# Attention and SwiGLU on one core: the first unit's k cut in three around the first scores, DMA transposes ahead of the q/k loads, the second weight slice's loads at fixed points

## The chip, the core and the metric

The kernel runs on one NeuronCore of a Trainium2 chip. The engines named here are TensorE (PE; its weight loads are listed apart as PEld), VectorE (DVE), ScalarE (ACT), GpSimd (POOL) and SyncE (SP), which only issues transfers to the 16 DMA engines. The metric is device microseconds (us) of one execution. Before: 575.25 us, the median of three runs (572.65, 576.69, 575.25).

## The reference

Four batches of twelve heads with 448 positions and 64 columns go through a sigmoid attention; the result, normalized by its root mean square, goes through a SwiGLU block (768 to 1536 to 768):

```python
scores = scale * np.matmul(q, k.transpose(0, 1, 3, 2)) - np.log(S)
attn = 1.0 / (1.0 + np.exp(-scores))
attn_out = np.matmul(attn, v)
x = attn_out.transpose(0, 2, 1, 3).reshape(B * S, H * D)
xn = x / np.sqrt(np.mean(x * x, axis=-1, keepdims=True) + 1e-06) * rms_g
g, val = xn @ w_gate, xn @ w_val
out = (g / (1.0 + np.exp(-g)) * val) @ w_out
```

All inputs and the output are float32. The kernel keeps that precision by splitting each operand into a high and a low float16 half and taking three products of halves.

## The kernel before, in words

**Units and chunks.** The attention is cut into 12 units of four heads. A unit has 7 chunks of 64 key rows per head. For each chunk PE makes the scores (line 277, 12 matmuls in float16 halves), ACT puts the sigmoid on them (line 281), and two chunks later PE multiplies by v (line 292, 8 matmuls in float32). The loop takes chunks in pairs: two chunks of scores, then the two `av` products of the pair before. The loop variable `n` counts chunks in steps of two, so unit u begins at chunk 7u: unit 4 with `n` = 28, unit 7 in the second chunk of `n` = 48.

**How q and k reach PE.** Scores need q and k with the head column on the partitions, while the loads bring positions there. A unit's raw q or k is loaded by two transfers, one per head pair (line 190). DVE makes the halves (`qk_hi`, line 222, and `qk_lo`, line 226, two instructions). From unit 3 on one DMA transpose on SP turns all four halves of a unit (`transpose_both`, line 229; 28 blocks of 128x128 in float16). Units 1 and 2 use PE for all or part of it (`on_pe`, line 258). Unit 0 is turned on PE in float32 (`transpose_here`, line 247): q in two pieces of 4 and 3 blocks, then k the same way; each piece is evicted by ACT (line 251, the high half) and DVE (line 252, the low half). Ahead of that and between q and k, PE does filler matmuls (`warm`, line 871).

**What sets the order.** Nothing is scheduled by a tool: each engine runs its instructions in the order in which the code issues them. `FILL[c]` lists what is issued at chunk c of every unit u. Before, chunk 3 issues `qk_lo` of q for unit u+2 and then the k load for unit u+4; chunk 4 issues the q load for unit u+4 and then the DMA transposes for unit u+2. SP's queue takes these strictly in that order, and a transfer that waits holds all that stand behind it. A transfer also waits for the one issued eight earlier.

**Weights.** The weights of gate and value come in six slices of 256 columns. A slice has six loads (line 459; one of 384 KB and two of 192 KB for gate, the same for value). DVE rebuilds float32 from the words loaded (lines 439 to 441), forms differences (line 491), ACT and DVE make halves (lines 494, 497). The second slice's loads enter a list once DVE has been given the first slice. Before, the attention loop takes `n // LOADS_FROM` of the list at the end of every pair from n = 10 on; the split of the second slice is issued from n = 30 on.

**Normalization.** After a batch's three units, PE sums squares (`ssq`, line 349), DVE makes the inverse root (lines 354 to 377), PE spreads it over the partitions (`rinv`, line 387), ACT evicts it (line 388), and DVE scales x and makes sums and differences (lines 391, 413) whose halves ACT (line 395) and DVE (line 402) write. These parts stand in a list that is drained between chunks in an order fixed by costs in the code; each engine's order is thus fixed in the program, and they come ahead of the parts that split the weights only as their turn allows. The SwiGLU part (line 527 and later) follows.

Of the kernel before, what the change touches and what calls it, by code (L numbers as in the profile page):

```python
# [12 lines left out]
AF = mybir.ActivationFunctionType  # L13
ALU = mybir.AluOpType


SQ = 2.0**6
# [7 lines left out]
def attention_then_swiglu(  # L25
# [21 lines left out]
    nc = tc.nc  # L47
    B, H, S, D = q.shape
    DFF, DM = w_out.shape
    P = 128  # L50
    NPAIR = H // 2
    NSLOT = 2 * S // P
# [14 lines left out]
    ps_s = ctx.enter_context(tc.tile_pool(name="ps_s", bufs=2, space=bass.MemoryType.PSUM))  # L67
    ps_m = ctx.enter_context(tc.tile_pool(name="ps_m", bufs=4, space=bass.MemoryType.PSUM))

    WARM, BETWEEN = 6, 2  # L70
    SPLIT_AT, REST_AT = (8, 30), 12
    LOADS_FROM = 10
    NAT = (0, 2, 0, 1, 2, 0, 1, 2, 0, 1, 0, 1)
    PIECES = (0, 4), (4, 3)
    MID = 3
    SLOT = 0.8
    ACT_SLOT = 0.18

# [7 lines left out]
    ident = const.tile([P, P], F32, name="ident")  # L86
# [38 lines left out]
    t_b = [words(xc_room, XW + (2 + n) * UW, 2, 2, NSLOT, P, dt=F16) for n in range(3)]  # L125
# [47 lines left out]
    def bank(name):  # L173
        return ps_m.tile([P, 512], F32, tag="m", name=name)
# [4 lines left out]
    stt = nc.vector.scalar_tensor_tensor  # L179
# [3 lines left out]
    at, pav = {}, {}  # L183
# [8 lines left out]
    def load_qk(u, t):  # L192
        load((q, k)[t], (raw_b if u < 2 else ld_b)[u % 2][:, t], u)

    def load_v(u):
        load(v, v_b[u % 2], u)

# [17 lines left out]
    def raw(u, t):  # L215
        return (raw_b if u < 2 else ld_b)[u % 2][:, t]
# [20 lines left out]
            in_=nat(u)[:, t].rearrange("p l c d -> p (l c d)"),  # L237
        )

    def transpose_here(u, t):  # L240
        src, dst = raw(u, t), t_b[u % 3][:, t]
        ps = [bank("tr") for _ in range(2)]
        for c in range(NSLOT):
            half_, at = divmod(c, MID + 1)
            for r in range(2):
                o = ps[half_][D * r : D * r + D, at * P : at * P + P]
                nc.tensor.matmul(o, src[:, r, c], ident, start=True, stop=True)  # L247
        for half_ in range(2):
            n = MID + 1 - half_
            hi, lo = (dst[:, l, half_ * (MID + 1) : half_ * (MID + 1) + n].rearrange("p c r -> p (c r)") for l in range(2))  # L250
            nc.scalar.activation(hi, ps[half_][:, : n * P], AF.Copy, scale=SQ)
            stt(lo, ps[half_][:, : n * P], SQ, hi, ALU.mult, ALU.subtract)

    def on_pe(u, t, begin, n):
        for l in range(2):
# [69 lines left out]
    def run_evictions(n):  # L325
        for part in evictions[:n]:
            part()
        del evictions[:n]
# [123 lines left out]
    loads = []  # L452
# [8 lines left out]
    def run_load():  # L461
        if loads:
            loads.pop(0)[1]()
# [364 lines left out]
    K, Q = 1, 0  # L828
# [9 lines left out]
    def from_1(n, part, *t, cost=0.0):  # L838
        run = ahead_by(n, part, *t, cost=cost)
        return lambda u: u and run(u)  # L840

    def first(*parts):
        return [only(0, x, *a, cost=cost) for x, *a, cost in parts]

    def second(*parts):
        return [only(1, x, *a, cost=cost) for x, *a, cost in parts]

    FILL = (
        first((qk_hi, 1, Q, 0.53), (qk_lo, 1, Q, 1.0)) + second((qk_hi, 2, Q, 0.53), (qk_lo, 2, Q, 1.0), (load_qk, 4, Q, 0.0), (on_pe, 1, K, *PIECES[1], 0.0)) + [from_1(2, qk_hi, K, cost=0.53)],
        first((qk_hi, 1, K, 0.53), (qk_lo, 1, K, 1.0)) + [from_1(2, qk_lo, K, cost=1.0)],  # L850
        [from_1(2, qk_hi, Q, cost=0.53)],
        first((on_pe, 1, Q, *PIECES[0], 0.0)) + [from_1(2, qk_lo, Q, cost=1.0), from_1(4, load_qk, K)],
        first((on_pe, 1, Q, *PIECES[1], 0.0), (qk_hi, 2, K, 0.53)) + [from_1(4, load_qk, Q), from_1(2, transpose_both)],
        first((on_pe, 1, K, *PIECES[0], 0.0), (qk_lo, 2, K, 1.0)) + second((on_pe, 2, Q, *PIECES[0], 0.0)),
        first((transpose, 2, K, 0.0), (load_qk, 4, K, 0.0)) + second((on_pe, 2, Q, *PIECES[1], 0.0)),
    )
# [8 lines left out]
    with tc.manual_schedule():  # L865
# [3 lines left out]
        def warm(n):  # L869
            for _ in range(n):  # L870
                nc.tensor.matmul(ps_w[:, :P], ones, ones, start=True, stop=True)  # L871

        warm(WARM)
        load_qk(0, Q)
        load_qk(0, K)
        load_v(0)
        load_qk(1, Q)
        load_qk(1, K)
# [8 lines left out]
            for _ in range(3):  # L887
                run_load()

        transpose_here(0, Q)  # L890
        warm(BETWEEN)
        transpose_here(0, K)

        todo = [(u, c) for u in range(NU) for c in range(NSLOT)]
        split = {}
        for n in range(0, len(todo) + 2, 2):
            for u, c in todo[n : n + 2]:
                scores(u, c)
                run_evictions(1)
                for part in FILL[c]:  # L900
                    part(u)
                if n == 6 and c == 6:
                    g_columns()
                run_later()
            for u, c in todo[max(n - 2, 0) : n]:
                av(u, c)
                run_evictions(1)
                run_later()
            for _ in range(n // LOADS_FROM):
                if loads and loads[0][0] < 2:  # L910
                    run_load()
            if n in SPLIT_AT:
                fc = SPLIT_AT.index(n)
                split[fc] = split_w(fc)
                first, second = split[fc]
                splits.extend(first[:4] if fc == 0 else first + second)
            if n == REST_AT:
                splits.extend(split[0][0][4:] + split[0][1])
# [49 lines left out]
        for fc, n in order:  # L968
# [5 lines left out]
            elif fc + 1 < NFC:  # L974
                first, second = split[fc + 1] = split_w(fc + 1) if n == 0 else split[fc + 1]
# [97 lines left out]
```

## Time and profile before

| what | value |
|---|---|
| median of three runs | 575.25 us (572.65 to 576.69) |
| the profiled execution | 576.9 us, span 575.1 us |
| PE busy | 565.1 us (98%), in 4230 instructions |
| DVE busy | 437.8 us (76%) |
| ACT busy | 265.7 us (46%) |
| chain that ended last | PE 90%, ACT 4%, DVE 2%, DMA 2% |
| attention (0 to 140 us) | PE busy 134.47 us, DMA share 0.92 |
| rest (140 to 575 us) | PE busy 430.64 us, DMA share 0.46 |

The profile is of one execution that took 576.9 us; its span is 1.8 us shorter. Times of rows count from the start of the span. A row of the timeline gives start, duration, engine, line, operation, result and operands, how many instructions are merged in it, and in brackets how long the engine was idle ahead of it and what ended the idle time. "SPq" rows are the time that SP took to issue a transfer; the landing is later and told by another view. PEclk is the granted clock of TensorE as a part of 2.4 GHz.

### The profile page before, as it was taken

Reading aid. Unit: us, or ns where it says so; the run is one execution under the profiler, and the core shown is the slowest. Engines: PE = TensorE matmul, PEld = TensorE weight load, DVE = VectorE, ACT = ScalarE, POOL = GpSimd, SP = SyncE. Lnnn points to the kernel's source line nnn. Section 1 sums busy time; section 2 is a strip of 40 time slices with the busy share of each in tenths; the row PEclk is TensorE's granted clock in tenths of the full one; section 3 lists DMA queues with packets and bytes.
Section 4 is the critical chain, followed back from the end, with each engine's and each line's share of the span. In section 5 each row is a group of like instructions: output and inputs, shape, how many; then the busy total and the mean of one; then the engine's idle time right before and its main releaser. Section 6 shows DMA issues by size and latency. Waiting matters only on the chain.

```text
span 575.1 us, 10260 instructions
## 1 busy us (share of the span) xinstructions
PE 565.1 (98%) x4230; PEld 304.9 (53%) x4230; DVE 437.8 (76%) x576; ACT 265.7 (46%) x397; POOL 0.7 (0%) x6
## 2 busy tenths in 40 slices
PE   8998999999999999999999999999999999999997
PEld 6454554454555555555555555555556666666664
DVE  4786899998887777878778787787557987777751
ACT  5687698886454243342433424325438342222220
POOL 0000000000000000000000000000000000000000
PEclk9999899999999999999999999999999999999999
DMA  8999998980016357282563835632526566444211
GB/s 254 257 260 241 251 255 200 176 191 18 1 47 171 118 156 196 91 225 78 156 192 98 218 80 158 188 106 66 177 59 225 152 220 198 149 142 144 69 43 41
DMA packets 98417, 87.25 MB, mean 152 GB/s; under 512 B 38719, under 2 KB 91458, under 8 KB 98370
## 3 DMA queue, kind: packets, MB, share of 16 engines
q1 hardware_dynamic: 97810, 85.91, 56.0%
q8 instruction: 33, 0.54, 0.4%
q10 hardware_dynamic: 560, 0.69, 0.3%
q14 instruction: 14, 0.11, 0.1%
HBM read 61.34 MB, written 16.52 MB: 135 GB/s over the span
## 4 chain that ended last, share of the span: by engine, by line
PE 90%; ACT 4%; DVE 2%; DMA 2%; issue 1%; ACTq 0%; DVEq 0%
PE cb L527 28%; PE cd L527 14%; PE av L292 7%; PE oc L730 7%; PE od L730 7%; PE o L730 7%; PE ca L527 7%; PE sc L277 6%; PE ob L730 4%; ACT room L281 3%; DMA xc<-room 2%; PE ssq L349 1%; PE tr L247 1%; PE warm L871 1%; ACT wr L494 1%
## 5 line engine op out<-in xcount | busy, mean ns | idle before, releaser
L527 PEld LDWEIGHTS <-wr 128*128 128x128 f16 x1512 | 147.9, 98 | 138.6 <-issue 1.0
L527 PE MATMUL cb<-xc,wr 128*128 128x448 f16 x756 | 147.3, 352 | 0.0
L281 ACT ACTIVATE room<-sc 128x896 f32<-128x896 f32 x84 | 75.4, 934 | 18.5 <-PE sc L277 17.8
L292 PE MATMUL av<-room 64*64 64x448 f32 x672 | 72.4, 547 | 0.0
L527 PE MATMUL cd<-xc,wr 128*128 128x448 f16 x324 | 65.2, 352 | 0.0
L277 PE MATMUL sc<-xc 64*64 64x448 f16 x1008 | 58.6, 356 | 4.4 <-DMA xc<-room 2.3
L277 PEld LDWEIGHTS <-xc 64*64 64x64 f16 x1008 | 30.6, 108 | 37.1 <-issue 23.2
L582 DVE TENSOR_TENSOR room<-cd,room 128x448 f32<-128x448 f32 x24 | 15.0, 625 | 43.1 <-PE cd L527 43.1
L730 PEld LDWEIGHTS <-xc 128*128 128x128 f16 x360 | 35.2, 98 | 23.3
L497 DVE SCALAR_TENSOR_TENSOR wr<-wr 128x1536 f16<-128x1536 f32 (+3 forms) x28 | 37.3, 1355 | 10.7 <-ACT wr L494 10.7
L527 PE MATMUL ca<-xc,wr 128*128 128x448 f16 x216 | 44.8, 352 | 0.0
L730 PE MATMUL o<-room,wr 128*128 128x384 f16 x252 | 41.1, 326 | 0.0
L550 ACT ACTIVATE room<-cb 128x448 f32<-128x448 f32 x24 | 13.1, 544 | 53.8 <-PE cb L527 53.8
L292 PEld LDWEIGHTS av<-room 64*64 64x64 f32 x672 | 25.2, 135 | 23.3 <-issue 18.6
L571 ACT ACTIVATE room<-cb 128x448 f32<-128x448 f32 x24 | 13.1, 544 | 50.6 <-PE cb L527 30.6
L730 PEld LDWEIGHTS <-room 128*128 128x128 f16 x270 | 26.4, 98 | 17.5
L494 ACT ACTIVATE wr<-wr 128x768 f16<-128x768 f32 (+1 forms) x48 | 34.0, 761 | 0.0
L585 ACT ACTIVATE room<-room 128x448 f32<-128x448 f32 x24 | 13.8, 577 | 43.2 <-DVE room L582 43.2
L730 PEld LDWEIGHTS <-wr 128*128 128x128 f16 x252 | 24.7, 98 | 16.3
L685 ACT ACTIVATE xc<-xc 128x1536 f16<-128x1536 f32 (+1 forms) x12 | 14.5, 1260 | 35.7 <-DVE xc L682 35.7
L491 DVE TENSOR_TENSOR wr<-wr 128x384 f32<-128x384 f32 x48 | 26.5, 553 | 0.8
L543 ACT ACTIVATE room<-cb 128x448 f32<-128x448 f32 x24 | 13.1, 545 | 25.5 <-PE cb L527 25.5
(98 smaller groups left out, 681.3 us busy)
## 6 DMA issues: line engine op xcount, KB each, us to landing
y_d<-room SPq DMA_DIRECT2D x24, 448.0 KB, 3.2
xc<-in_moe_w_out_dram SPq DMA_DIRECT2D x12, 768.0 KB, 5.6
xc<-y_d SPq DMA_DIRECT2D x22, 384.0 KB, 4.4
room<-in_v_dram SPq DMA_DIRECT2D x24, 224.0 KB, 3.9
out_dram<-room SPq DMA_DIRECT2D x49, 96.0 KB, 2.2
wr<-in_moe_w_gate_dram SPq DMA_DIRECT2D x12, 384.0 KB, 4.2
wr<-in_moe_w_gate_dram SPq DMA_DIRECT2D x24, 192.0 KB, 4.8
wr<-in_moe_w_val_dram SPq DMA_DIRECT2D x12, 384.0 KB, 5.7
```

The lines of the kernel that those rows point to most:

```text
L277: nc.tensor.matmul(o, T[rows, 1, l, c, cols], T[rows, 0, m, :, cols], start=(n == 0), stop=(n == 2))
L281: nc.scalar.activation(a, ps[:, :, :S], AF.Sigmoid, bias=-math.log(S), scale=1.0 / (math.sqrt(D) * SQ * SQ))
L292: nc.tensor.matmul(ps[D * (j ^ r) : D * (j ^ r) + D, :S], v_b[u % 2][rows, r, c], a[rows, r], start=(c == 0), stop=(c == NSLOT - 1),)
L491: first.append((lambda o=o, f0=f0, f1=f1: tt(wf[:, o], wf[:, f0], wf[:, f1], ALU.subtract), 0.6))
L494: nc.scalar.activation(t[:, 0, s], wf[:, s], AF.Copy, scale=SW)
L497: stt(t[:, 1, s], wf[:, s], SW, t[:, 0, s], ALU.mult, ALU.subtract)
L527: nc.tensor.matmul(ps, w[:, l, b, c], xc[n, a][:, r, c], start=(not more and c == 0 and m == 0), stop=(c == NK - 1 and m == 2), skip_group ...
L543: nc.scalar.activation(y[:, 0], pb[:, :S], AF.Copy)
L582: tt(y[:, 1], pd[:, :S], y[:, 1], ALU.add)
L585: nc.scalar.activation(y[:, 1], y[:, 1], AF.Silu, scale=UNIT)
L685: return lambda: nc.scalar.activation(s[:, 0, a:b], f[:, a:b], AF.Copy), 0.0, ()
L730: nc.tensor.matmul(ps[:, :HALF], a(m, l), w(m, r), start=(not more and m == 0 and n == 0), stop=(m == NM - 1 and n == 2), skip_group_check ...
```

## The change

Three things change.

1. Unit 0's first loads are cut by blocks in place of head pairs: q in pieces of blocks 0-3 and 4-6, k in pieces of 0-1, 2-4 and 5-6, both head pairs in one transfer. PE turns q and the first piece of k, then runs the first chunk's scores; the second piece of k is turned behind chunk 0, the third behind chunk 1. The filler goes from six and two matmuls to five and none.
2. From unit 1 on, chunk 3 issues the DMA transposes of unit u+2, and chunk 4 the k and q loads of unit u+4.
3. The second weight slice's loads are taken at n = 18 and 20 (one each) and n = 26 and 28 (two each).

```diff
-    WARM, BETWEEN = 6, 2
+    WARM = 5
     SPLIT_AT, REST_AT = (8, 30), 12
-    LOADS_FROM = 10
+    LOADS_AT = {18: 1, 20: 1, 26: 2, 28: 2}
...
-    MID = 3
+    K_PIECES = (0, 2), (2, 3), (5, 2)
...
+    def load_first(t, *pieces):
+        rows = (q, k)[t][0, :4].rearrange("(r h) s d -> r (h s) d", r=2).rearrange("r (p c) d -> p r c d", p=P)
+        for begin, n in pieces:
+            nc.sync.dma_start(raw(0, t)[:, :, begin : begin + n], rows[:, :, begin : begin + n])
...
-    def transpose_here(u, t):
-        src, dst = raw(u, t), t_b[u % 3][:, t]
-        ps = [bank("tr") for _ in range(2)]
-        for c in range(NSLOT):
-            half_, at = divmod(c, MID + 1)
-            for r in range(2):
-                o = ps[half_][D * r : D * r + D, at * P : at * P + P]
-                nc.tensor.matmul(o, src[:, r, c], ident, start=True, stop=True)
...
+    def transpose_here(t, *pieces):
+        src, dst = raw(0, t), t_b[0][:, t]
+        ps = [bank("tr") for _ in pieces]
+        for o, (begin, n) in zip(ps, pieces):
+            for c in range(n):
+                for r in range(2):
+                    nc.tensor.matmul(
+                        o[D * r : D * r + D, c * P : c * P + P], src[:, r, begin + c], ident, start=True, stop=True
+                    )
+        for o, (begin, n) in zip(ps, pieces):
+            hi, lo = (dst[:, l, begin : begin + n].rearrange("p c r -> p (c r)") for l in range(2))
+            nc.scalar.activation(hi, o[:, : n * P], AF.Copy, scale=SQ)
+            stt(lo, o[:, : n * P], SQ, hi, ALU.mult, ALU.subtract)
...
-        first((qk_hi, 1, Q, 0.53), (qk_lo, 1, Q, 1.0)) + second(...
+        first((transpose_here, K, K_PIECES[1], 0.0), (qk_hi, 1, Q, 0.53), (qk_lo, 1, Q, 1.0)) + second(...
-        first((qk_hi, 1, K, 0.53), (qk_lo, 1, K, 1.0)) + [from_1(2, qk_lo, K, cost=1.0)],
+        first((transpose_here, K, K_PIECES[2], 0.0), (qk_hi, 1, K, 0.53), (qk_lo, 1, K, 1.0)) + [from_1(2, qk_lo, K, cost=1.0)],
...
-        first((on_pe, 1, Q, *PIECES[0], 0.0)) + [from_1(2, qk_lo, Q, cost=1.0), from_1(4, load_qk, K)],
-        first((on_pe, 1, Q, *PIECES[1], 0.0), (qk_hi, 2, K, 0.53)) + [from_1(4, load_qk, Q), from_1(2, transpose_both)],
+        first((on_pe, 1, Q, *PIECES[0], 0.0)) + [from_1(2, qk_lo, Q, cost=1.0), from_1(2, transpose_both)],
+        first((on_pe, 1, Q, *PIECES[1], 0.0), (qk_hi, 2, K, 0.53)) + [from_1(4, load_qk, K), from_1(4, load_qk, Q)],
...
-        load_qk(0, Q)
-        load_qk(0, K)
+        load_first(Q, *PIECES)
+        load_first(K, *K_PIECES)
...
-        transpose_here(0, Q)
-        warm(BETWEEN)
-        transpose_here(0, K)
+        transpose_here(Q, *PIECES)
+        transpose_here(K, K_PIECES[0])
...
-            for _ in range(n // LOADS_FROM):
-                if loads and loads[0][0] < 2:
-                    run_load()
+            for _ in range(LOADS_AT.get(n, 0)):
+                run_load()
```

On SP, between the transposes of unit 3 and those of unit 4, this stood before (`in_k`, `in_q`: loads of unit 6; `in_v`: units 3 and 4):

```order
L229 DMA_TRANSPOSE xc<-room 128x28x128
L459 DMA wr<-in_moe_w_gate_dram 128x3x256
L459 DMA wr<-in_moe_w_gate_dram 64x3x256
L190 DMA room<-in_v_dram 128x448 x2
L459 DMA wr<-in_moe_w_gate_dram 64x3x256
L190 DMA xc<-in_k_dram 128x448 x2
L459 DMA wr<-in_moe_w_val_dram 128x3x256
L190 DMA xc<-in_q_dram 128x448 x2
L229 DMA_TRANSPOSE xc<-room 128x28x128
L459 DMA wr<-in_moe_w_val_dram 64x3x256 x2
L190 DMA room<-in_v_dram 128x448 x2
```

The last transpose of these rows is that of unit 4. In the changed kernel the transposes of unit 4 come first of the following rows, and the second transpose is that of unit 5:

```order
L234 DMA_TRANSPOSE xc<-room 128x28x128
L190 DMA xc<-in_k_dram 128x448 x2
L190 DMA xc<-in_q_dram 128x448 x2
L464 DMA wr<-in_moe_w_gate_dram 128x3x256
L464 DMA wr<-in_moe_w_gate_dram 64x3x256
L190 DMA room<-in_v_dram 128x448 x2
L234 DMA_TRANSPOSE xc<-room 128x28x128
L190 DMA xc<-in_k_dram 128x448 x2
L190 DMA xc<-in_q_dram 128x448 x2
L464 DMA wr<-in_moe_w_gate_dram 64x3x256
L464 DMA wr<-in_moe_w_val_dram 128x3x256
L190 DMA room<-in_v_dram 128x448 x2
```

Behind these stand the last two value loads of the second slice and then the transposes of unit 6. The third gate load and all value loads have moved behind the transposes of unit 5; between the transposes of units 3 and 4 only q, k and v loads are left.

On ACT, from the first eviction on, before (lines 251 and 281 are the evictions of turned pieces and the sigmoids of chunks):

```order
L251 ACTIVATE xc<-tr 128x512
L251 ACTIVATE xc<-tr 128x384
L251 ACTIVATE xc<-tr 128x512
L251 ACTIVATE xc<-tr 128x384
L281 ACTIVATE room<-sc 128x896 x4
```

And in the changed kernel (lines 256 and 286):

```order
L256 ACTIVATE xc<-tr 128x512
L256 ACTIVATE xc<-tr 128x384
L256 ACTIVATE xc<-tr 128x256
L286 ACTIVATE room<-sc 128x896
L256 ACTIVATE xc<-tr 128x384
L286 ACTIVATE room<-sc 128x896
L256 ACTIVATE xc<-tr 128x256
L286 ACTIVATE room<-sc 128x896 x2
```

The sigmoid of chunk 0 has moved ahead of two of k's three evictions, that of chunk 1 ahead of one. On DVE the low half of k's third piece now stands behind the halves of unit 1's q; after these first rows the orders of PE, ACT and DVE are the same as before.

## Rows read from the trace of the kernel before

**Rows 1.** The chain that ended last, 36 to 64 us: start, us, what.

```profile
44.62 9.59 DMA xc<-room
```

**Rows 2.** PE's timeline of the attention, around unit 4 and a later pair.

```profile
50.25 1.70 PE L292 MATMUL av<-room 64*64 64x448 f32 x16
54.25 1.82 PE L277 MATMUL sc<-xc 64*64 64x448 f16 x24 [2.30 <-DMA xc<-room]
...
62.33 1.67 PE L292 MATMUL av<-room 64*64 64x448 f32 x16
...
88.41 1.70 PE L292 MATMUL av<-room 64*64 64x448 f32 x16
...
90.92 1.33 PE L277 MATMUL sc<-xc 64*64 64x448 f16 x24
92.07 1.67 PE L292 MATMUL av<-room 64*64 64x448 f32 x16
```

**Rows 3.** Windows of 1 us: busy by engine, PEclk, DMA share, GB/s.

```profile
55.00:56.00 1.00, 1.00 (x20) 0.59 (x12) 0.00 (x0) 0.88 (x1) 0.00 (x0) 0.50 1.03 256
```

**Rows 4.** SP's timeline, 30 to 60 us: time to issue.

```profile
36.75 1.23 SPq L459 DMA_DIRECT2D wr<-in_moe_w_gate_dram  x2
...
41.55 1.02 SPq L190 DMA_DIRECT2D xc<-in_k_dram  x2
...
44.62 6.09 SPq L229 DMA_TRANSPOSE xc<-room  x1
...
56.46 5.84 SPq L229 DMA_TRANSPOSE xc<-room  x1
```

**Rows 5.** Line 229, the transposes: issue ns min/median/max, and us to landing.

```profile
L229 SPq DMA_TRANSPOSE xc<-room x9: 4225/5777/6705, 30.4 to 116.5; - x9
...
DMA to landing us min/median/max: 6.1/8.6/8.9
```

**Rows 6.** DMA issues of 20 to 60 us: count, KB each, median us to landing.

```profile
wr<-in_moe_w_gate_dram SPq DMA_DIRECT2D x2, 192.0 KB, 5.2
```

**Rows 7.** DVE's timeline, 24 to 142 us.

```profile
38.14 1.15 DVE L226 SCALAR_TENSOR_TENSOR room<-xc,room 128x448 f16<-128x448 f32 x2
...
59.18 0.16 DVE L354 TENSOR_SCALAR m<-ssq 112x4 f32<-112x4 f32 x1 [6.17 <-PE ssq L349]
...
62.32 0.55 DVE L439 TENSOR_SCALAR wr<-wr 128x768 uint32<-128x768 uint32 x1
...
65.31 0.55 DVE L439 TENSOR_SCALAR wr<-wr 128x768 uint32<-128x768 uint32 x1
...
70.82 1.55 DVE L391 TENSOR_TENSOR room<-room 128x1344 f32<-128x1344 f32 x1
...
84.95 1.56 DVE L402 TENSOR_TENSOR xc<-room,xc 128x1344 f16<-128x1344 f32 x1 [1.17 <-ACT xc L395]
...
131.72 1.56 DVE L391 TENSOR_TENSOR room<-room 128x1344 f32<-128x1344 f32 x1 [2.94 <-ACT room L388]
```

**Rows 8.** ACT's timeline, 60 to 160 us.

```profile
75.76 1.06 ACT L395 ACTIVATE xc<-room 128x448 f16<-128x448 f32 x2
...
131.15 0.54 ACT L388 ACTIVATE room<-rinv 128x448 f32<-128x448 f32 x1
```

**Rows 9.** All engines' timeline of the start: PE and ACT.

```profile
1.08 2.93 PE L871 MATMUL warm<-ones 128*128 128x128 f32 x12 [1.08 <-DVE ones L860]
...
3.94 3.26 PE L247 MATMUL tr<-ident,room 128*64 128x128 f32 x28
...
7.25 0.49 ACT L251 ACTIVATE xc<-tr 128x384 f16<-128x384 f32 x1 [0.68 <-PE tr L247]
...
7.77 1.75 PE L247 MATMUL tr<-ident,room 128*64 128x128 f32 x28
...
8.91 1.15 ACT L251 ACTIVATE xc<-tr 128x512 f16<-128x512 f32 x2 [1.17 <-PE tr L247]
...
10.72 3.50 ACT L281 ACTIVATE room<-sc 128x896 f32<-128x896 f32 x4 [0.67 <-PE sc L277]
```

More of the change, by code (lines that the diff above doesn't have):

```diff
@@ L238, in transpose @@
         )
-    def transpose_here(u, t):
-        src, dst = raw(u, t), t_b[u % 3][:, t]
-        ps = [bank("tr") for _ in range(2)]
-        for c in range(NSLOT):
-            half_, at = divmod(c, MID + 1)
-            for r in range(2):
-                o = ps[half_][D * r : D * r + D, at * P : at * P + P]
-                nc.tensor.matmul(o, src[:, r, c], ident, start=True, stop=True)
[L248 to L252, printed above, removed]
+    def transpose_here(t, *pieces):
[11 more added lines that the diff above has]
+            stt(lo, o[:, : n * P], SQ, hi, ALU.mult, ALU.subtract)
     def on_pe(u, t, begin, n):
@@ L848, in attention_then_swiglu @@
     FILL = (
-        first((qk_hi, 1, Q, 0.53), (qk_lo, 1, Q, 1.0)) + second((qk_hi, 2, Q, 0.53), (qk_lo, 2, Q, 1.0), (load_qk, 4, Q, 0.0), (on_pe, 1, K, *PIECES[1], 0.0)) + [from_1(2, qk_hi, K, cost=0.53)],
-        first((qk_hi, 1, K, 0.53), (qk_lo, 1, K, 1.0)) + [from_1(2, qk_lo, K, cost=1.0)],
+        first((transpose_here, K, K_PIECES[1], 0.0), (qk_hi, 1, Q, 0.53), (qk_lo, 1, Q, 1.0)) + second((qk_hi, 2, Q, 0.53), (qk_lo, 2, Q, 1.0), (load_qk, 4, Q, 0.0), (on_pe, 1, K, *PIECES[1], 0.0)) + [from_1(2, qk_hi, K, cost=0.53)],
+        first((transpose_here, K, K_PIECES[2], 0.0), (qk_hi, 1, K, 0.53), (qk_lo, 1, K, 1.0)) + [from_1(2, qk_lo, K, cost=1.0)],
         [from_1(2, qk_hi, Q, cost=0.53)],
-        first((on_pe, 1, Q, *PIECES[0], 0.0)) + [from_1(2, qk_lo, Q, cost=1.0), from_1(4, load_qk, K)],
-        first((on_pe, 1, Q, *PIECES[1], 0.0), (qk_hi, 2, K, 0.53)) + [from_1(4, load_qk, Q), from_1(2, transpose_both)],
+        first((on_pe, 1, Q, *PIECES[0], 0.0)) + [from_1(2, qk_lo, Q, cost=1.0), from_1(2, transpose_both)],
+        first((on_pe, 1, Q, *PIECES[1], 0.0), (qk_hi, 2, K, 0.53)) + [from_1(4, load_qk, K), from_1(4, load_qk, Q)],
         first((on_pe, 1, K, *PIECES[0], 0.0), (qk_lo, 2, K, 1.0)) + second((on_pe, 2, Q, *PIECES[0], 0.0)),
```

## The prediction, made before the changed kernel ran

> **What bounds the kernel now.** I read the page's table of engines first (PE is busy nearly all the time), then the chain of waits for the places where the end hangs on something else, then the timelines of PE, SP and DVE around them. Apart from the start, one stop of PE is worth much. The chain puts 9.59 us on a transfer issued at 44.62 [rows 1]: the DMA transposes of unit 4. PE's product with v that starts at 50.25 is over at 51.95; the next scores, unit 4's first, start at 54.25, 2.30 us later [rows 2].
>
> The stop costs more than its gap. One microsecond later the granted clock reads 0.50, the lower of TensorE's levels, 1.2 GHz [rows 3]. From 54.25 to the product at 62.33, 8.08 us pass [rows 2]; in them stand 24 score matmuls, 16 with v, the 8 of the sum of squares and 24 score matmuls. At the full clock the last three took 92.07 - 88.41 = 3.66 us and 24 score matmuls 92.07 - 90.92 = 1.15 us [rows 2], together 4.81 us. The lower clock cost 8.08 - 4.81 = 3.27 us. **The stop and what follows it: 5.6 us.**
>
> Were those transposes late because their data was? DVE had finished unit 4's last half at 38.14 + 1.15 = 39.29 [rows 7]. The transposes were issued 5.3 us after that: SP was issuing loads of k, q and weights that stand ahead of them [rows 4]. The queue's order made them late.
>
> **Part 1, the start.** Removed: one of six filler matmuls, 2.93/6 = 0.49 us, and the two between q and k [rows 9]. Ahead of chunk 0, PE now turns 4 of k's 14 blocks: 1.75 x 4/14 = 0.50 us in place of 1.75, or 0.93 at q's slower rate (3.26 x 4/14) [rows 9]. q's turning then starts near 3.5 and ends near 6.7, k's first piece is through near 7.5; one eviction of 256 columns (ACT 0.38 us, from 0.49 for 384 and 0.58 for 512 [rows 9]) and its low half on DVE follow, and chunk 0's sigmoid can start near 8.75 in place of 10.72. But ACT now has two evictions between the first four sigmoids: 0.49 + 0.38 + 3.50 = 4.37 us, so the fourth ends near 13.1 against 14.22 before [rows 9]. DVE is held alike: unit 1's halves stand behind the low half of k's second piece, and PE turns unit 1's q ahead of its first product with v. So of 2.0 us at the first sigmoid about 1.1 us are left at the fourth. I take **1.0 us**; ends 0 (k's pieces land late) and 2.0 us.
>
> Smaller pieces may land later. The loads' time before is shown only whole. The Trainium skill, "Perfetto Trace Analysis", section "DMA Optimizations", says that larger transfers use the bandwidth better and that splitting helps when the DMA engines are generally idle; no row of mine shows pieces of this size, and by that rule this term would be 0 and the forecast 1.0 us later.
>
> **Part 2, the transposes of unit 4.** Ahead of them on SP stand now unit 3's transposes, k and q of unit 5 and v of unit 3. SP had its first weight load behind such a set at 36.75 [rows 4]; with v, about 1.0 us, it is free at 37.7, before DVE's 39.29. So DVE decides: with the start's 1.0 us, 38.3. Landing takes 8.6 us, 8.9 at most [rows 5]: 46.9 to 47.2. PE comes to unit 4 at 51.95 - 1.0 = 50.95. Nearly 4 us of room: the stop goes, and with it the fall of the clock. **PE then runs 5.6 + 1.0 = 6.6 us earlier** from 62 on, if nothing else holds it.
>
> **Part 3, what is late next.** Two things were pushed back. Unit 6's q and k are now issued from 44.4 to 46.4; with 5.2 us to landing, as for a gate load of about that size [rows 6], they are there by 51.6, and DVE is done with them about 1.8 us later (a high half of some 0.6 and two low halves, 1.15 [rows 7]), at 53.4. I cost that at nothing, since DVE's next work waits for PE until 53.8 (below); without that cover it would cost 1.4 us against the 52.0 at which DVE would have been done. The weights matter. SP after 38.3: transposes 6.09, k and q of unit 6 at 1.02 each, two gate loads 1.23, v 1.0, unit 5's transposes 5.84, k and q of unit 7 at 1.02 each [rows 4]: the third gate load is issued near 56.5 and lands 5.2 us later [rows 6], at 61.7. With both transposes at their shortest issue of 4.2 us [rows 5], 58.2. DVE could use it earlier: before, it sat idle for 6.17 us waiting for the sum of squares, and began on the gate slice at 62.32, 3.1 us after the wait ended at 59.18 [rows 7]. Now that sum ends later than 50.95 by 24 score matmuls, 1.15, and by 16 products with the sum, 90.92 - 88.41 = 2.51 [rows 2], less eight products, half of 1.70: at 53.8. DVE asks for the gate slice at 56.9. It waits 1.3 to 4.8 us. The value loads land some 2.7 us behind and are asked for 65.31 - 62.32 = 3.0 us behind [rows 7]: no further wait.
>
> So DVE gains not 5.4 us but 62.32 - 61.7 = 0.6 to 62.32 - 58.2 = 4.1 us. I take 2.6, nearer the long end, as transposes with fewer loads ahead of them should issue in less than 6 us.
>
> Does PE wait for DVE? Twice through ACT. ACT's halves of x at 75.76 need DVE's product of 70.82, done at 72.37 [rows 7, 8]: 3.4 us of slack. PE 6.6 us and DVE 2.6 us earlier eat 4.0 of it: ACT stops for 0.6 us, and PE, fed by ACT's sigmoids there, keeps 6.0 us. At the end of the attention DVE's wait for `rinv` was 2.94 us [rows 7], of which the eviction takes 0.54 [rows 8] and PE's matmuls about as much, so 1.8 us are slack; DVE's wait for ACT of 1.17 us at 84.95 [rows 7] closes too. The gain there is the smaller of 6.0 and 2.6 + 1.17 + 1.8 = **5.6 us**. Behind that PE's work and DVE's order are unchanged, so the gain stays.
>
> The sum: 576.9 - 5.6 = **571.3 us**. It is made against the profiled execution, 1.65 us above the median of 575.25; against the median the gain is 4.0 us, 0.7%. By the same steps DVE at 4.1 gives 6.6 (570.3); at 0.6 the third rival's mechanism sets in.
>
> **The rivals.**
> - *All of it is kept (0.20).* The transposes take long on SP only because loads are queued ahead; moved ahead, they take 4.2 us, the weights come at 58.2 and PE keeps 6.6 us: 570.3; with the start's upper end 569.3. For: the issue times range from 4.2 to 6.7 us for the same 28 blocks [rows 5]. Against: the two nearest took 5.84 and 6.09 [rows 4]. The Trainium skill, "DMA: Bandwidth & Descriptors", section "Latency and other measured facts", gives DMA transposes 261 GB/s: as an estimate, 3.5 us for a unit's 0.92 MB, which speaks for this case.
> - *The start gains nothing (0.12).* k's pieces land late or DVE's first halves hold PE: 572.3.
> - *The weights come so late that the run is slower (0.10).* ACT stops at 75.76 for PE's lead less DVE's less 3.4 us. Before, a gap of 2.30 us was followed by the lower clock [rows 2, 3]. If ACT's stop opens such a gap, 3.3 us more are lost. That happens when DVE's gain is under 0.9 us, the third gate load landing after 61.4. At 63.5 DVE is 1.2 us late, ACT stops for 4.4, and PE is left with 6.6 - 4.4 - 3.3 = -1.1: 578.0. It is slower from about 62.4 on. For: my long end is 61.7. Against: it needs every transfer slow.
> - *It doesn't do what it says (0.06).* Another transfer holds SP, unit 4's transposes still land after PE has come, and only the start is gained: 575.9.
>
> **Numbers.** Forecast 0.52, with a range of its own of 569.5 to 573.5 (the start between 0 and 2.0 us, DVE between 1.5 and 4.1). Predicted 571.3. From 568.8 to 575.0 the range takes in the forecast, its bounds, the dead start and most of "all kept", and leaves out most of the 0.10 and the 0.06. A measurement of this kernel tells about 1% from no change: 5.75 us, below 569.5 or above 581.0. Faster by more needs nearly all of "all kept" with a good start, or the forecast's tail: 0.16. Slower by more needs DVE over 4 us late: 0.04. Within 1%: 0.80.
>
> **What would show it.** PE's timeline has no wait for a transfer at unit 4's first scores and the granted clock stays at 1.00 from 50 to 62 us. Chunk 0's sigmoid starts near 8.75, the first product with v near 12.7. SP issues unit 4's transposes near 38.3, the third gate load near 55. DVE waits for that load at its first pass over the slice (near 57 to 60), in place of its 6.17 us wait for the sum of squares. PE's first matmul of the SwiGLU comes 5 to 6 us earlier. I am wrong if PE stops elsewhere for a transpose, if the clock falls again, or if DVE's wait for weights lasts over 5 us.

## The result, and the profile of the changed kernel

The change made the kernel slightly slower: 578.09 us, the median of 16 runs (575.18 to 579.57), against 574.57 for the kernel before beside it (571.68 to 577.19). The ratio is 1.0056, 95% interval [1.0038, 1.0073]: 0.56% slower, less than the 1% taken as no change. The forecast was 571.3, with a range from 568.8 to 575.0: the measured time lies above all of it.

| | before, profiled | before, a second profile (f4 below) | changed, profiled |
|---|---|---|---|
| span, us | 575.1 | 572.0 | 575.4 |
| PE stop at unit 4's first scores | 2.30 | 1.87 | none |
| first `rinv` matmul at | 66.58 | 62.99 | 60.07 |
| second `ssq` at | 90.04 | 86.95 | 89.87 |
| fourth `ssq` at | 141.86 | 138.77 | 142.13 |
| from there to the end of the span | 433.24 | 433.23 | 433.27 |

The last line says where to look: behind the attention nothing changed. PE was 6.5 us ahead of the first profile at 60 us and level with it at 90. PE's timeline of the changed kernel (columns as in [rows 2]):

```profile
12.99 1.73 PE L297 MATMUL av<-room 64*64 64x448 f32 x16
...
50.99 1.33 PE L282 MATMUL sc<-xc 64*64 64x448 f16 x24
...
54.69 1.31 PE L282 MATMUL sc<-xc 64*64 64x448 f16 x24
55.82 1.68 PE L297 MATMUL av<-room 64*64 64x448 f32 x16
57.32 1.31 PE L282 MATMUL sc<-xc 64*64 64x448 f16 x24
...
60.07 0.55 PE L392 MATMUL rinv<-room,ones 112*128 112x448 f16 x2
...
66.20 0.97 PE L297 MATMUL av<-room 64*64 64x448 f32 x4 [0.92 <-DMA room<-in_v_dram]
67.63 0.59 PE L297 MATMUL av<-room 64*64 64x448 f32 x2 [0.46 <-DMA room<-in_v_dram]
...
76.93 1.57 PE L282 MATMUL sc<-xc 64*64 64x448 f16 x24 [3.05 <-ACT room L286]
...
89.87 0.95 PE L354 MATMUL ssq<-ones,room 128*112 128x1 f32 x8 [0.52 <-DVE room L322]
```

Unit 4's first scores (50.99) follow the product with v without a bracket: the stop of [rows 2] is gone, and the product that stood at 62.33 is at 55.82. Then three new waits: 0.92 and 0.46 us for v, and 3.05 us for ACT. From `rinv` to the second `ssq` PE now takes 29.80 us in place of 23.46; these waits are 4.4 of the 6.3 us. DVE shows what ACT waited for:

```profile
53.99 0.16 DVE L359 TENSOR_SCALAR m<-ssq 112x4 f32<-112x4 f32 x1 [0.85 <-PE ssq L354]
...
63.04 0.56 DVE L444 TENSOR_SCALAR wr<-wr 128x768 uint32<-128x768 uint32 x1 [5.83 <-DMA wr<-in_moe_w_gate_dram]
...
68.36 0.56 DVE L444 TENSOR_SCALAR wr<-wr 128x768 uint32<-128x768 uint32 x1 [2.24 <-DMA wr<-in_moe_w_val_dram]
...
73.45 1.55 DVE L396 TENSOR_TENSOR room<-room 128x1344 f32<-128x1344 f32 x1
```

The 6.17 us for the sum of squares in [rows 7] have become 0.85; in their place DVE stands 5.83 us at the gate slice and 2.24 at the value slice. Its second product with the inverse root, which ACT's halves read, ends at 75.00, against 70.82 + 1.55 = 72.37 in [rows 7]. ACT's timeline has the other end of it; it starts at 75.03 what stood at 75.76 in [rows 8], then without a wait:

```profile
75.03 1.04 ACT L400 ACTIVATE xc<-room 128x448 f16<-128x448 f32 x2 [3.08 <-DVE room L396]
```

SP's timeline says why the weights came then:

```profile
38.60 5.76 SPq L234 DMA_TRANSPOSE xc<-room  x1
...
47.67 1.94 SPq L190 DMA_DIRECT2D room<-in_v_dram  x2
49.71 6.04 SPq L234 DMA_TRANSPOSE xc<-room  x1
...
56.90 1.66 SPq L190 DMA_DIRECT2D xc<-in_q_dram  x2
58.59 0.63 SPq L464 DMA_DIRECT2D wr<-in_moe_w_gate_dram  x1
...
60.91 1.69 SPq L464 DMA_DIRECT2D wr<-in_moe_w_val_dram  x2
```

Unit 4's transposes go out at 38.60 in place of 44.62 [rows 4]. The third gate load goes out at 58.59, after DVE has begun to ask for it (63.04 - 5.83 = 57.21), and the last value loads behind the load of v.

### The profile page after: what moved, and what is told of

The parts are those of the page before. It is cut to its first block, busy times and chain, and to the rows that moved or that the text cites. A ratio compares the mean times of both kernels' runs of the same rounds, so it can differ in the third digit from the quotient of the medians.

```text
span 575.4 us, 10231 instructions
## 1 busy us (share of the span) xinstructions
PE 562.7 (98%) x4224; PEld 306.1 (53%) x4224; DVE 437.9 (76%) x577; ACT 265.7 (46%) x398; POOL 0.7 (0%) x6
## 4 chain that ended last, share of the span: by engine, by line
PE 90%; DVE 5%; DMA 2%; ACT 1%; issue 1%; SPq 0%; DVEq 0%; ACTq 0%
PE cb L532 28%; PE cd L532 14%; PE av L297 7%; PE oc L735 7%; PE od L735 7%; PE o L735 7%; PE ca L532 7%; PE sc L282 6%; PE ob L735 4%; DMA wr<-in_moe_w_val_dram 1%; DVE room L231 1%; DVE room L396 1%; DVE room L322 1%; ACT room L286 1%; PE tr L251 1%
## 5 line engine op out<-in xcount | busy, mean ns | idle before, releaser
L297 PE MATMUL av<-room 64*64 64x448 f32 x672 | 73.7, 538 | 1.4 <-DMA room<-in_v_dram 1.4
L282 PE MATMUL sc<-xc 64*64 64x448 f16 x1008 | 59.8, 351 | 4.9 <-ACT room L286 4.2
L282 PEld LDWEIGHTS <-xc 64*64 64x64 f16 x1008 | 32.2, 106 | 34.9 <-issue 24.2
L297 PEld LDWEIGHTS av<-room 64*64 64x64 f32 x672 | 27.1, 133 | 24.2 <-issue 16.8
```

Of the source, the lines that this page charges most:

```text
L282: nc.tensor.matmul(o, T[rows, 1, l, c, cols], T[rows, 0, m, :, cols], start=(n == 0), stop=(n == 2))
L297: nc.tensor.matmul(ps[D * (j ^ r) : D * (j ^ r) + D, :S], v_b[u % 2][rows, r, c], a[rows, r], start=(c == 0), stop=(c == NSLOT - 1),)
```

## The experiments

Theory: the lead is lost because the second weight slice comes too late, DVE stops for it, then ACT, then PE. Rivals: the order of transposes, the cut start, or a general backlog of transfers. All ratios are against the kernel before in the same session.

### One part at a time: e1 to e4

e1 has part 1 of the change alone, e2 part 2 alone, e3 part 3 alone, e4 parts 1 and 2. For e2 and e3 the edits of the kernel before are:

```diff
 e2
-  ... from_1(4, load_qk, K)],   ... [from_1(4, load_qk, Q), from_1(2, transpose_both)],
+  ... from_1(2, transpose_both)],   ... [from_1(4, load_qk, K), from_1(4, load_qk, Q)],
 e3
-            for _ in range(n // LOADS_FROM):
+            for _ in range(LOADS_AT.get(n, 0)):
```

> Only the start is changed (unit 0's k in three pieces, five filler matmuls); FILL and the takes of the second slice's loads are those of before. All theories: the product with v of chunk 0 starts about 0.75 us earlier, as in the changed kernel (12.99 against 13.74). Unit 4's transposes still stand behind loads on SP, so the stop at unit 4 stays and eats part of it. Expected against before: -0.3 us (-1.0 to +0.5), ratio 0.998 to 1.001.

> Only FILL is changed: transposes at chunk 3, k and q loads at chunk 4; start and takes of before. Theory L (the second slice's loads, pushed behind unit 5's transposes, cost what the change wins): the stop at unit 4 is gone, DVE waits for no weight load at its first passes over the second slice, and the run is 5 us shorter than before (3 to 6.5, ratio 0.989 to 0.995). Rival O (the new order of transposes, k, q and v itself makes transfers late): PE or DVE wait for transfers between 60 and 80 us all the same, ratio 0.998 to 1.006. Rival N (what PE wins is given back to DVE before the attention ends, whatever the loads do): no wait for weights, yet the sum of squares of the last batch starts at the same time as before within 1.5 us, ratio 0.997 to 1.003.

> Only the takes are changed (n = 18, 20, 26, 28); start and FILL of before, so unit 4's transposes stand behind k and q of unit 6 but ahead of all weight loads of the second slice. Theory L: the stop at unit 4 is shorter or gone, DVE waits several us for gate and value loads, and the run is no faster than before: +2 us (0 to +4, ratio 1.000 to 1.007). Rival O: no wait for weights above 1 us and a gain of 3 to 6 us. Rival N: within 1.5 us of before.

> The whole change but for the takes of the second slice's loads, which are those of before. Theory L: 6 us shorter than before (4 to 7.5, ratio 0.987 to 0.993), no wait for weights on DVE, none for v on PE. Rival O: waits between 60 and 80 us stay, ratio 0.999 to 1.006. Rival N: PE comes to unit 4 without a stop, but the last sum of squares is no more than 1.5 us earlier, ratio 0.997 to 1.003.

The mean clock of a run is TensorE's granted clock over the whole execution, as a part of 2.4 GHz. Every profile here whose run has a mean clock of 0.997 or less shows windows at 0.50 in the attention or just behind it; the profiles at 0.998 or more show none there. The last column counts such runs.

| | median, us | ratio to before | stop at unit 4 | waits for weights (DVE) | runs at 0.997 or less |
|---|---|---|---|---|---|
| before (stops of two profiles) | 574.25 | | 2.30 and 1.87 | none | 10 of 35 |
| e1 start | 575.03 | 1.0018 [0.9999, 1.0036] | 2.34 | none | 9 of 12 |
| e2 order | 573.26 | 0.9984 [0.9964, 1.0004] | none | none | 0 of 12 |
| e3 points | 575.91 | 1.0026 [1.0008, 1.0044] | none | 5.48 and 1.03 | 10 of 12 |
| e4 start and order | 574.32 | 1.0003 [0.9987, 1.0019] | none | none | 2 of 12 |
| all three | 578.09 | 1.0056 [1.0038, 1.0073] | none | 5.83 and 2.24 | 14 of 16 |

Only e3 came out as theory L expected. e1 is just above its range. For e2 and e4 theory L expected 5 and 6 us less than before; e4 shows no gain, and e2 gains 0.9 us with an interval that takes in 1. So the late weight slice explains why the change is slower than before, and only part of why the forecast gain is missing.

Part 2 and part 3 each take the stop away. Part 2 takes the k and q loads of unit 6 and a value load from ahead of unit 4's transposes (issued at 38.48 in e2, with three gate loads still ahead of them), part 3 takes the weight loads away (41.56 in e3). Together they clear the same stop twice. The points cost 0.53% on top of e4. They alone bring the waits for weights, in e3's profile with a stop of PE for ACT of 3.57 us. e2's price is another: its v and k are late (PE's timeline, then DVE's; e4's waits are alike, 1.09 and 0.67 us for v and 3.72 us for k):

```profile
57.56 2.06 PE L292 MATMUL av<-room 64*64 64x448 f32 x14 [1.25 <-DMA room<-in_v_dram]
```

```profile
53.47 0.63 DVE L222 TENSOR_SCALAR room<-xc 128x896 f16<-128x896 f32 x1 [4.55 <-DMA xc<-in_k_dram]
```

### Without the slice, and with its loads on another engine: f1 to f4

```diff
 f1
+        if fc != 1:
             loads.extend((fc, lambda d=d, x=x: nc.sync.dma_start(d, x)) for ...
 f2 (changed kernel), f3 (kernel before)
+        queue = nc.gpsimd if fc == 1 else nc.sync
-        loads.extend((fc, lambda d=d, x=x: nc.sync.dma_start(d, x)) for ...
+        loads.extend((fc, lambda d=d, x=x: queue.dma_start(d, x)) for ...
```

> The changed kernel without the six loads of the second weight slice (DVE then works on whatever words stand there, so that slice's part of the output is left out). Theory (the lead of 6.5 us is lost to transfers that come late, because SP has more to issue between 27 and 75 us than time for it): 4.0 us of issue time go from SP, DVE's waits of 5.83 and 2.24 us for weights and PE's waits of 0.92 and 0.46 us for v go, ACT no longer stops PE for 3.05 us, the sum of squares of the second batch stands at 84 to 86 us in place of 89.9, and the kernel takes 571 to 573.5 us, 4 to 7 below the changed kernel. Rival (the lead is lost to ACT or DVE themselves, whatever the loads do): the sum of squares stays at 88.5 to 90.5 and the time within 1.5 us of the changed kernel's.

> The changed kernel with the second weight slice's six loads issued by GpSimd in place of SP; the same bytes are moved. Theory (SP's issue time is what is short): no wait of DVE for weights over 1 us, unit 5's and 6's transposes issued 2 to 4 us earlier, waits of PE for v gone, 571.5 to 573.5 us, 4 to 6 below the changed kernel. Rival (the DMA engines' bandwidth is short, their share being above 1.0 there): the loads only push other transfers back; transposes or k land late by some 4 us, PE or DVE wait for those instead, and the time stays at 575.5 to 578.

> The kernel before, its order kept, with the second slice's six loads issued by GpSimd in place of SP. Theory (SP's issue time): some 4 loads with 2.4 us or more of issue time go from ahead of unit 4's transposes, which are issued near 41.5 in place of 44.62 and land near 50.5; PE's stop of 2.3 us at 51.95 goes without any reordering, nothing else gets late, and the time is 571 to 573. Rival (bandwidth): the transposes are issued earlier but take as much longer to land, the stop stays above 1.5 us, and the time is within 1 us of before.

> The kernel before, unchanged, a second profile of it. Theory (the lower clock after the stop comes only in some of its executions, so that the forecast counted 3.27 us that most runs do not have): if this execution's mean clock is 0.999 or more, PE's stop for unit 4's transposes is there with 2 to 2.6 us, but the granted clock stays at 1.00 and the first matmul that spreads the inverse root stands near 63.3 in place of 66.6. Rival (the fall follows from every such stop): the granted clock reads 0.50 near 55 us again and that matmul stands at 66 to 67.

f1: 570.18 us, ratio 0.9936 [0.9912, 0.9959], on the theory's side and a little past it. Even without the slice the gain is 0.64%, some 3.7 us, and not the forecast 5.6. PE keeps the lead; the second sum is 7.45 us earlier than in the changed kernel:

```profile
58.97 0.55 PE L392 MATMUL rinv<-room,ones 112*128 112x448 f16 x2
...
82.42 0.95 PE L354 MATMUL ssq<-ones,room 128*112 128x1 f32 x8
```

f2 and f3: 585.90 us, 1.0216 [1.0172, 1.0260], and 585.40 us, 1.0207 [1.0180, 1.0235]. Both forms of the theory are wrong here, and the rival is too small. In f2 GpSimd sent all six loads between 28.10 and 36.39, during unit 3's transposes; SP had sent them between 46.46 and 62.60 in the changed kernel. So they went out from another engine and also much earlier. SP's row of f2, PE's, and the window of 30 to 50 us (columns as in [rows 3]):

```profile
28.48 14.92 SPq L234 DMA_TRANSPOSE xc<-room  x1
```

```profile
53.27 1.34 PE L282 MATMUL sc<-xc 64*64 64x448 f16 x12 [13.13 <-DMA xc<-room]
```

```profile
30.00:50.00 20.00, 10.14 (x148) 4.99 (x148) 10.74 (x18) 10.17 (x15) 2.19 (x4) 0.85 1.15 142
```

The issue of unit 3's transposes took 14.92 us in place of 6.77 in the changed kernel, so "SP's time to issue" is no fixed price: it grew with what else was under way. The DMA engines were as busy as in the same window of the changed kernel (1.15 in both) and moved 142 GB/s in place of 241. The Trainium skill, "DMA: Bandwidth & Descriptors", section "Issuing engines are not separate DMA queues", says that transfers started by different engines run on the same 16 DMA engines and interleave; the trace agrees that sending from elsewhere saved nothing, and adds that throughput fell. Whether any second engine would do that, GpSimd alone, or the earlier time was not told apart, so f2 and f3 do not settle what the bytes cost on SP's queue; g1 below was made for that.

f4: 573.82 us; PE's timeline, and the window that answers to [rows 3]:

```profile
50.34 1.70 PE L292 MATMUL av<-room 64*64 64x448 f32 x16
53.91 1.33 PE L277 MATMUL sc<-xc 64*64 64x448 f16 x24 [1.87 <-DMA xc<-room]
...
86.95 0.95 PE L349 MATMUL ssq<-ones,room 128*112 128x1 f32 x8
```

```profile
55.00:56.00 1.00, 1.00 (x17) 0.25 (x9) 0.00 (x0) 1.00 (x2) 0.00 (x0) 1.00 1.04 308
```

The same kernel, the same stop, a little shorter, and the granted clock stays at 1.00. PE is at `rinv` at 62.99, 3.6 us earlier than in the profile on which the prediction rests. The expectation asked for a mean clock of 0.999 and this run has 0.998, but the place in question had no fall. The profile of before had 0.993. Of the 35 runs of the kernel before in the session of e1 to e4, 10 had 0.997 or less, with a median of 575.00 us; the other 25 have 573.29. The fall was in a minority of executions, and it is worth 1.0 us of the median of all (574.25). e2, without a run at 0.997 or less, has 573.26: its small gain is what those 25 runs of before have already.

### Small loads, and loads put late: g1 to g4

```diff
 g1 (changed kernel): d[: min(8, ...)], x[: min(8, ...)] in the second slice's six loads
 g2 (changed kernel), g3 (kernel before), g4 (part 2 alone)
-    SPLIT_AT, REST_AT = (8, 30), 12
+    SPLIT_AT, REST_AT = (8, 46), 12
+    LOADS_AT = {36: 1, 38: 1, 40: 1, 42: 1, 44: 2}
```

> The changed kernel with each of the second slice's six loads cut to 8 partitions (24 KB in place of 384 or 192; the rest of that slice's words is whatever stands there): as many transfers, in the same places of the queue, a tenth of the bytes. Theory (the DMA engines' time for the bytes is what is short; SP only shows the backlog): as without the loads, 569.5 to 571.5 us, no wait of DVE for weights over 0.5 us, second sum of squares near 82.5. Rival (SP's time to issue, or the places in the queue): most of the six loads' issue time stays, waits for v or weights of 1 us and more stay, and the time is 573 to 576.

> The changed kernel with the second slice's loads at n = 36, 38, 40, 42 (one each) and 44 (two), and its split from n = 46 on in place of 30; nothing is left out. Theory (the bytes are too many between 25 and 75 us, and cost less where ACT holds PE and after unit 11's loads are out): up to 70 us PE runs as without the loads (spreading of the first inverse root at 59 to 60), later stops of PE come to under 2 us, 570 to 573 us. Rival (the six loads cost the same wherever they stand, since every unit fills the DMA engines): the stops come 15 to 25 us later and the time is 575 to 578.

> The kernel before, its start and its order of transposes and loads kept, with the loads and the split of the second slice as late as in g2. Theory (bytes, not order): unit 4's transposes are issued near 41.5 in place of 44.4 and land by 50.5, PE does not stop for them at 52, 570.5 to 573 us. Rival (the order of transposes and q/k loads matters by itself): PE still stops over 1 us for transposes, 573.5 us or more.

> Part 2 alone (transposes ahead of the q and k loads) with the loads and the split of the second slice as late as in g2. Theory (bytes): within 1 us of g2 and of g3, 570 to 573 us. Rival (order): over 1.5 us from one of them, faster than g3 if early transposes help, slower than g2 if the cut start helps.

g1: 572.41 us, 0.9970 [0.9948, 0.9991], just between the two expectations. With as many transfers in the same places, a tenth of the bytes takes away some 0.86% of the kernel before, 4.9 us of the 6.9 that f1 takes away against the changed kernel. The bytes (and the packets that carry them, which fell with them) are most of it. The other 2 us, loosely measured with intervals of this width, are left to the places. DVE still waits for the third gate load:

```profile
59.77 0.57 DVE L444 TENSOR_SCALAR wr<-wr 128x768 uint32<-128x768 uint32 x1 [2.52 <-DMA wr<-in_moe_w_gate_dram]
```

g2, g3, g4: 591.38, 587.59 and 591.78 us; ratios 1.0296 [1.0278, 1.0314], 1.0227 [1.0207, 1.0248], 1.0301 [1.0282, 1.0319]. The theory's first half held: PE runs without a stop over 1 us up to the first `rinv` in all three, with `rinv` at 59.88, 60.73 and 60.66. The second half failed by 15 to 19 us: my points were too late for a split at n = 46, and a later split costs by itself (h1 below); the two were not told apart. g2's DVE, then PE:

```profile
82.91 0.56 DVE L444 TENSOR_SCALAR wr<-wr 128x768 uint32<-128x768 uint32 x1 [3.78 <-DMA wr<-in_moe_w_gate_dram]
92.18 0.56 DVE L444 TENSOR_SCALAR wr<-wr 128x768 uint32<-128x768 uint32 x1 [6.18 <-DMA wr<-in_moe_w_val_dram]
...
95.13 0.16 DVE L359 TENSOR_SCALAR m<-ssq 112x4 f32<-112x4 f32 x1
```

```profile
95.34 1.01 PE L297 MATMUL av<-room 64*64 64x448 f32 x2 [8.97 <-DVE m L359]
```

The mechanism is the case's own in large: a DVE that stands at a weight load holds what is queued behind it, here the reading of the second sum, and PE's next product waits for that for 8.97 us.

### DVE asks later: h1 to h4, i1, i2

h1 and i1 are the changed kernel with the split from n = 34 on, so that the scaling of x stands ahead of it on DVE; SP's queue is unchanged. h2 also takes the loads behind v; h3 is h2 without the cut start; h4 is the changed kernel, i2 is e2 again.

```diff
-    SPLIT_AT, REST_AT = (8, 30), 12
+    SPLIT_AT, REST_AT = (8, 34), 12
 h2, h3
+    LOADS_AT = {22: 3, 28: 3}
```

> The changed kernel with the split of the second slice from n = 34 on in place of 30; SP's transfers and their order are unchanged, and DVE scales x ahead of it. Theory (a), that DVE's waits for weights give PE's lead back: no wait of DVE for weights over 1 us, DVE's first scaling near 61 in place of 66 to 68, the stop of PE for ACT of 3.05 us near 77 is under 1 us, the waits for v stay near 1.4 us in all, second sum of squares at 84 to 86, 572 to 574 us. Rival (b, c), that the backlog of transfers holds PE whoever waits: stops of PE of over 3 us in all between 60 and 90, second sum of squares at 88 or later, 575.5 us or more.

> h1 with the loads taken three at n = 22 and three at n = 28, so that v of units 4 and 5 stands ahead of them, and the transposes of units 5 and 6 behind all three. If (b), the order behind k and q, made v late: the waits for v go, 571 to 573 us, 1 us or more below h1. If (c), the backlog only moves: the transposes of unit 5 land later than PE asks (near 61) and PE waits 1 us or more for them or for weights; the time is h1's or above.

> Part 2 alone (the start as before) with the split from n = 34 on and the loads as in h2. If the cut start is worth its 0.75 us at the first product with v, 0.5 to 1 us above h2; if it costs (PE asks earlier than transfers come), the same as h2 or up to 1 us below.

> The changed kernel, unchanged, for the comparison on the same chip: by all theories 576.5 to 579 us, with DVE's waits for weights over 4 us and PE's stop for ACT over 2 us, and a mean clock under 0.999 in most executions.

> h1 unchanged, a second profile. If the backlog of transfers decides (c), this execution shows a stop of PE of 1.5 us or more for a transfer (v or transposes) between 60 and 90 us that h1's first profile did not have, and takes 577 us or more; if the later split alone costs (more DVE work left for the SwiGLU), PE runs up to 85 us as in h1 and the difference stands behind 85 us.

> Part 2 alone, unchanged, timed again. If taking away unit 4's stop is worth what a before without the lower clock loses there (1.87 us, less the 1.25 us wait for v that e2 showed), 0.9985 to 0.9995; if it was chance, 1.000 or above.

| | median, us | ratio to before | second `ssq` at | from the fourth `ssq` to the end |
|---|---|---|---|---|
| h1 | 578.73 | 1.0082 [1.0051, 1.0114] | 84.56 | 435.58 |
| i1 (one run) | 580.74 | | 87.51 | 437.29 |
| h2 | 577.94 | 1.0082 [1.0052, 1.0113] | 89.30 | 437.33 |
| h3 | 578.18 | 1.0074 [1.0045, 1.0103] | 84.78 | 437.29 |
| h4 | 578.63 | 1.0082 [1.0051, 1.0113] | 93.84 | 433.24 |
| i2 | 573.44 | 0.9986 [0.9966, 1.0005] | 86.31 | 433.27 |

h1's profile shows the chain of waits cut: no wait of DVE for weights, no stop of PE for ACT over 0.7 us, the second sum at 84.56, 5.3 us earlier than in the changed kernel, with the same transfers. So the stop of PE for ACT came by way of DVE's early ask. PE's waits for v are absent from this profile too, which the later split does not explain; in i1, where they are present, the second sum is at 87.51, 2.4 us earlier than in the changed kernel, again without a stop for ACT over 0.7 us. Yet the time did not fall, and the expectation (572 to 574) is missed. PE's timeline of h1:

```profile
84.56 0.95 PE L354 MATMUL ssq<-ones,room 128*112 128x1 f32 x8
...
88.74 0.59 PE L297 MATMUL av<-room 64*64 64x448 f32 x2 [1.58 <-DVE m L359]
...
95.49 0.55 PE L392 MATMUL rinv<-room,ones 112*128 112x448 f16 x2
...
145.15 0.36 PE L392 MATMUL rinv<-room,ones 112*128 112x448 f16 x1 [2.05 <-DVE room L382]
```

The work that DVE put off stands in the way twice: before the second inverse root (10.9 us from sum to `rinv`, 7.2 in the changed kernel), and before the fourth, where the stretch behind the attention grows from 433.3 to 435.6. In i1, h2 and h3 the lower clock follows there as well. i1 is another execution of h1's program, and its PE waits for v, as theory (c) would have it:

```profile
67.13 0.97 PE L297 MATMUL av<-room 64*64 64x448 f32 x4 [1.32 <-DMA room<-in_v_dram]
68.50 0.59 PE L297 MATMUL av<-room 64*64 64x448 f32 x2 [0.40 <-DMA room<-in_v_dram]
```

Both expected branches of i1 came true in part: waits for a transfer of 1.72 us in all between 60 and 90 us, though no single one of 1.5, and a price behind 85. h2's early v brought no gain: its profile waits 2.63 us for v of a later unit, and the lower clock follows (0.50 from 80 to 82 us). h3 is no faster or slower than h2 within their intervals. h4 repeats the changed kernel with longer waits (7.98 us for the gate slice, 4.32 for ACT).

i2: 573.44 us, 0.9986 [0.9966, 1.0005], inside what was expected. Yet twice part 2 alone was nominally 0.15% faster than before and twice the interval took in 1. It beats the changed kernel; that it beats the kernel before is not shown. No other version that loads the whole slice did better.

## Why the prediction was wrong, point by point

- **The price of the stop, 5.6 us: mis-sized.** The gap was read rightly; the 3.27 us for the lower clock were taken as part of every run. f4 has a stop of 1.87 us and no fall, and 25 of 35 runs of before have a mean clock that leaves no room for one. Against f4 the lead at `rinv` is 62.99 - 60.07 = 2.9 us, not 6.5. The warning stood in the prediction: the profiled execution was 1.65 us above the median.
- **Part 1, 1.0 us: right in its place, not in the time.** The first product with v came at 12.99 (13.74 in the profile before), 0.75 us; chunk 0's sigmoid at 8.99 against 8.75 foreseen. Yet e1's median shows no gain. Its first product comes at 12.68 and unit 4's first scores at 53.22, 1.0 us earlier than in the profile of before, but PE still waits for the transposes there, and the lower clock follows (PE's timeline, then the window that answers to [rows 3]):

```profile
53.22 1.76 PE L282 MATMUL sc<-xc 64*64 64x448 f16 x24 [2.34 <-DMA xc<-room]
```

```profile
55.00:56.00 1.00, 1.00 (x8) 0.01 (x1) 0.00 (x0) 0.93 (x2) 0.00 (x0) 0.50 1.02 376
```

  With 9 of 12 runs at a mean clock of 0.997 or less, against 10 of 35 before, a fall that comes more often would eat the gain. That is likely, not shown.
- **Part 2, the transposes of unit 4: right.** Issued at 38.60 against 38.3; no stop, no fall of the clock from 50 to 62 us.
- **Part 3, DVE's gain of 2.6 us: the step that failed.** DVE asked at 57.2, as foreseen (56.9). The third gate load was issued at 58.59, not 56.5: v took 1.94 us to issue, not 1.0, and q 1.66, not 1.02. Though it landed within 4.4 us and not 5.2, DVE's wait ended at 63.04, 1.3 us past my long end of 61.7. I took 59.7, "nearer the long end", and was not near enough. The 1.0 for v has no row behind it in the prediction. In the trace of before v took 0.99 us at 53.09, and right behind gate loads, where the change has it, 2.73; with that the long end is 63.4:

```profile
38.07 2.73 SPq L190 DMA_DIRECT2D room<-in_v_dram  x2
```

  And "the value loads land some 2.7 us behind ... no further wait" was wrong: DVE had them 5.3 us behind, after 2.24 us of wait. The last was issued 3.4 us behind the gate load and took 6.3 us to land. DVE's second product came 2.6 us later than before, where I had it 2.6 us earlier.
- **v itself was put at nothing.** The sum has no wait of PE for v; PE waited 0.92 and 0.46 us for it, in h4 2.09, and f1's profile, without the slice, has no such wait.
- **The third rival, given 0.10, is what happened.** Its condition was a third gate load after 61.4; at 63.5 it gave a stop of ACT of 4.4 us and 578.0. Measured: 63.04, 3.08 and 578.09. Its fall of the clock is not in the profile of the changed kernel, but that is its one run at 0.999; 14 of 16 have 0.997 or less. h4's profile shows one behind the stop for ACT:

```profile
81.00:82.00 1.00, 1.00 (x12) 0.67 (x15) 1.00 (x2) 1.00 (x2) 0.00 (x0) 0.50 1.16 213
```

  That 578.0 comes so close is luck. The rival had DVE 1.2 us late (its product was 2.6 late), nothing for v, 3.3 us for the clock where the profile has none, and a start from 576.9, a run of before with the fall. Its mechanism deserved more weight: my own bounds for the load, 58.2 to 61.7, were sums of short issue times for q and v.
- **"All of it is kept" rested on short transposes.** The two took 5.76 and 6.04 us to issue, against the 4.2 of that rival; issues near 4.2 us appear in g1 from 70 us on. The Trainium skill, "DMA: Bandwidth & Descriptors", section "Latency and other measured facts", gives 261 GB/s, as an estimate 3.5 us for these blocks; no issue of 28 blocks in these traces was that short, and the shortest took 4.13 us (g4).

Under all of it lies a balance I did not work out. A unit moves 6 transfers of 224 KB for q, k and v and 896 KB of transposes, 2.29 MB. PE takes 2.63 us for two chunks (54.69 to 57.32), 9.2 us for a unit's seven, so the units alone ask for about 249 GB/s. The DMA engines gave this, from 20 to 75 us, in f4 and in the changed kernel:

```profile
20.00:75.00 55.00, 52.27 (x757) 26.67 (x753) 47.14 (x83) 45.18 (x66) 0.00 (x0) 1.00 1.16 257
```

```profile
20.00:75.00 55.00, 51.95 (x734) 27.57 (x727) 41.86 (x75) 42.37 (x62) 0.00 (x0) 1.00 1.12 237
```

They are busy throughout (1.16 and 1.12). Without the slice (f1) the units alone moved nearly what the sum above asks for:

```profile
20.00:75.00 55.00, 54.41 (x796) 28.62 (x792) 49.95 (x86) 48.04 (x73) 0.00 (x0) 1.00 1.07 241
```

The second slice's 1.57 MB is some 6 us more at such a rate. An order of the queue can choose who waits: PE for transposes (before), PE and DVE for v and k (e2), or DVE and PE for weights and v (the change); none of the orders tried has a place where nobody does. That this balance is the bound is argued, not shown: f1, g1 and the reordered variants agree with it. The rate is no fixed ceiling either, since one stretch of before had 351 GB/s (56 to 59 us). A kernel with more DMA throughput, which would prove it, was not tried.

What stays open: whether some other placing of the six loads gains more than e2's 0.15%, what part of g2 to g4 is the later split, and why the same wait brings the lower clock in one execution and not in the next.

## What to carry to other kernels

Before pricing a reordered queue, add up the bytes of a stage and divide by what the DMA engines gave in it; if that fills the stage, expect that moving a transfer forward moves another back, and the work is to find whose wait is cheapest. Follow each displaced transfer to the in-order engine that asks for it and to what stands behind it there. Take the time to issue a transfer from the same place in the queue, not from a quiet one: v took 0.99 and 2.73 us in one trace. A clock fall in one profile is not a property of the kernel: look at the mean clock of the other runs before counting on getting it back.

## What the runs showed of the hardware that was not expected

- A stop is not always followed by the lower clock. 2.30 us in the profile of before and 2.34 in e1 were, 1.87 in f4 and 3.05 in the changed kernel were not, 4.32 in h4 was. h1 and i1 are one program with the same wait of 2.05 us at 145 and 148 us; the window behind it (first h1, 147 to 148 us, then i1, 150 to 151 us):

```profile
147.00:148.00 1.00, 1.00 (x7) 0.54 (x6) 1.00 (x1) 0.00 (x0) 0.00 (x0) 1.00 0.00 0
```

```profile
150.00:151.00 1.00, 1.00 (x5) 0.34 (x4) 1.00 (x1) 0.00 (x0) 0.00 (x0) 0.50 0.00 0
```

- The same DMA transpose of 28 blocks took from 4.13 us (g4) to 15.95 us (f3) to issue. The longest two, 14.92 in f2 and 15.95 in f3, are those beside GpSimd's loads.
- Loads sent by GpSimd during DMA transposes went with a DMA rate of 142 GB/s from 30 to 50 us in f2 and 190 in f3, against 241 in the changed kernel and 257 in the profile of before in the same window, at a busy share of 1.15 and 1.12 against 1.15 and 1.07.
